# Output products of the first eight units of a fused retention and MoE kernel: one plain float32 matmul in place of three reduced-precision ones

## The chip, the cores and the metric

The kernel runs on one core of a Trainium2 chip. The metric is the time of one execution on the device in microseconds; the median of several runs is compared. The engines are TensorE (PE; its weight loads are PEld), VectorE (DVE), ScalarE (ACT), GpSimd (POOL) and SyncE (SP, which issues all DMAs). Each works through its own instructions in order and waits on semaphores for the others.

## The reference

Three layers follow one another. A retention layer over 4 sequences of 768 positions, 8 heads of 64 features, gives 3072 tokens of 512 features. Then come two feed-forward layers; the change is in the first of them:

```python
def _moe_ref(x, w_in, w_out):            # x 3072x512, w_in 512x2048, w_out 2048x512
    h = x @ w_in
    g = h * (1.0 / (1.0 + np.exp(-1.702 * h)))
    return (g @ w_out).astype(np.float32)
...
    gate = 1.0 / (1.0 + np.exp(-(x @ w_gate)))     # second layer, d_ff 1536
    return (gate * (x @ w_val) @ w_out).astype(np.float32)
```

The feed-forward weights come as float64 words in memory; the kernel turns them into float32 itself.

## The kernel before

The first feed-forward layer works on six blocks of 512 tokens and sixteen slices of 128 of the 2048 features. A pair of block and slice is a **unit**; there are 96. The list `units` orders them: block 0 with slices 0 to 7, block 1 with slices 0 to 7, block 0 with 8 to 15, block 1 with 8 to 15, and then blocks 2 to 5 with all sixteen each. `FH` is 8, so units 0 to 7 are block 0 with the first eight slices. The order of all instructions is written by hand.

The precise products are made of three matmuls in the reduced-precision type float32r: an operand is split into a high part (a cast on ScalarE) and a low part (the difference, on VectorE or GpSimd), and high times high, high times low and low times high are added up in PSUM. Weights are split anew for each unit: `split_w` casts `wh` on ScalarE (line 265) and subtracts `wl` on GpSimd or VectorE (line 266). The float32 weights themselves stay in `raw1` for the whole layer. Attention products (`emit_scores`, `emit_update`, `emit_y`) are plain float32 matmuls; the profile records each of these as two instructions.

One turn of the loop over units issues, for unit i:

1. `conv[0]`, `conv[1]`: the first steps of turning weight tiles from float64 to float32, two tiles per unit in units 0 to 7 and one in the next ones: a scaling on ScalarE (line 228, tile `cva`, three buffers), then on VectorE L233 and L236.
2. `proj`: twelve matmuls of 512 columns into a bank `h` (L273 to L275).
3. `split_for(i + 1)`: the next unit's input weights, `wh` on ScalarE and `wl` on GpSimd (on VectorE from unit 24).
4. `gated`: a sigmoid on ScalarE (L279, into `sg`), the product with `h` on VectorE (L280), and the cast of its high part `gh` on ScalarE (L283).
5. `split_out(i + 1)`: the output weights of unit i - 1, `wh` on ScalarE and `wl` on GpSimd.
6. `conv[2]`: L242 and L246 on VectorE.
7. One item of attention for the next block, if there is one. Units 0 to 5 have two items each for block 1. A step of attention (128 tokens) is three items: scores (L144, masked on VectorE at L148), state (L165), and the output (L178, L185, evicted to `xh` on ScalarE and `xl` on VectorE, L190), which also prepares `vs` and `qs` of the following step on GpSimd (L110, L118).
8. `gated_lo`: the low part `gl` on VectorE (L288).
9. `conv[3]`: the sum that ends the conversion, on GpSimd (L256, into `raw1`).
10. `stage`: loads of further weight tiles. Then the second item of attention.
11. `emit_out(i - 2)`: the output product of the unit before the last, twelve matmuls of 512 columns (L365 to L367), four banks `acc` that add up over eight slices.

The banks `h` are three, taken in turn by the projections and the attention items. The tiles `gh` and `gl` have three buffers each, `sg` two.

Of the kernel before, what the change touches and what calls it, by code (L numbers as in the profile page):

```python
# [8 lines left out]
F32 = mybir.dt.float32  # L9
# [6 lines left out]
P = 128  # L16
# [8 lines left out]
def retention_moe_moe2(  # L25
# [12 lines left out]
    nc = tc.nc  # L38
# [12 lines left out]
    def pool(stack, name, bufs, side, **kw):  # L51
        return stack.enter_context(tc.tile_pool(name=name, bufs=bufs, side=side, reuse_waits="tile", **kw))
# [5 lines left out]
    g_p = pool(left, "g", 2, "left")  # L58
# [10 lines left out]
    def psum_tile(kind, shape=(P, 512)):  # L69
        i = turn[kind][0]  # L70
        turn[kind].rotate(-1)
        return psum[i].tile(list(shape), F32, name=kind, tag="bank")
# [121 lines left out]
    raw1 = {}  # L194
# [7 lines left out]
    def stage(n=1):  # L202

        for _ in range(min(n, len(to_stage))):
            ph, f, k = to_stage.popleft()
            t = cv_p.tile([P, 512], U64, name="w64", tag="w64", bufs=4)
            nc.sync.dma_start(out=t, in_=(w1 if ph == "1" else w2)[f, k])
            staged.append((ph, f, k, t))
# [53 lines left out]
    def split_w(raw, lo_engine):  # L262
        wh = wsp_p.tile([P, 512], F32R, name="wh", tag="wh")
        wl = wsp_p.tile([P, 512], F32R, name="wl", tag="wl")
        nc.scalar.copy(wh, raw)  # L265
        lo_engine.tensor_tensor(out=wl, in0=raw, in1=wh, op=ALU.subtract)  # L266
        return wh, wl


    def proj(bank, w, xh, xl, n):  # L270
        wh, wl = (a.rearrange("p (k f) -> p k f", k=KC) for a in w)
        for k in range(KC):
            nc.tensor.matmul(bank[:, :n], wh[:, k, :], xh[:, k, :n], start=(k == 0), stop=False)  # L273
            nc.tensor.matmul(bank[:, :n], wh[:, k, :], xl[:, k, :n], start=False, stop=False)  # L274
            nc.tensor.matmul(bank[:, :n], wl[:, k, :], xh[:, k, :n], start=False, stop=(k == KC - 1))  # L275

    def gated(bank, n):
        sg = g_p.tile([P, 512], F32, name="sg", tag="sg")
        nc.scalar.activation(out=sg[:, :n], in_=bank[:, :n], func=AF.Sigmoid, scale=1.702)  # L279
        nc.vector.tensor_tensor(out=sg[:, :n], in0=bank[:, :n], in1=sg[:, :n], op=ALU.mult)  # L280
        gh = g_p.tile([P, 512], F32R, name="gh", tag="gh", bufs=3)
        gl = g_p.tile([P, 512], F32R, name="gl", tag="gl", bufs=3)
        nc.scalar.copy(gh[:, :n], sg[:, :n])  # L283
        return sg, gh, gl

    def gated_lo(g, n):
        sg, gh, gl = g
        nc.vector.tensor_tensor(out=gl[:, :n], in0=sg[:, :n], in1=gh[:, :n], op=ALU.subtract)  # L288

    x_t, w_t, g_t, acc_t, half_t = {}, {}, {}, {}, {}  # L290
# [4 lines left out]
    def att_items(j):  # L295

        t0, n = blocks1[j]
        items = []
        for i in range(n // C):
            s = t0 // C + i  # L300

            def first(s=s, i=i):
                if i == 0:
                    alloc_x(j)
                emit_scores(s)
                if s >= 3:
                    load_next(s + 1, KN, V)

            def second(s=s):
                emit_update(s)  # L310
                if s >= 3:
                    load_next(s + 2, Q, K)

            def third(s=s, i=i):
                if s + 1 < NSTEP:
                    emit_prep(s + 1)
                emit_y(s, *x_t[j], i * C)

            items += [first, second, third]
        return deque(items)  # L320
# [3 lines left out]
    FH = F1 // 2  # L324
    segments = [(b, f0, f0 + FH) for f0 in (0, FH) for b in range(2)]
    segments += [(b, 0, F1) for b in range(2, len(blocks1))]
    units = [(b, f) for b, f0, f1 in segments for f in range(f0, f1)]
    starts = {(b, f0) for b, f0, f1 in segments}
    ends = {(b, f1 - 1) for b, f0, f1 in segments}
    DEPTH = 2  # L330

    def split_out(i):

        j = i - DEPTH
        if 0 <= j < len(units):
            w_t[j, "out"] = split_w(raw1[units[j][1], 1], nc.gpsimd)

    def split_for(i):

        if i < len(units):  # L340
            b, f = units[i]
            w_t[i, 0] = split_w(raw1[f, 0], nc.gpsimd if i < 3 * FH else nc.vector)

    def half_tile(c):
        if c < 3:
            return in_p.tile([P, 512], F32, name="half", tag="half", bufs=3)
        return g_p.tile([P, 512], F32, name="ost", tag="ost")

    def emit_out(i):
        b, f = units[i]  # L350
        if (b, f) in starts:
            acc_t[b] = [psum_tile("acc") for _ in range(4)]
            if f:
                half_t[b] = []
                for c in range(4):
                    half_t[b].append(half_tile(c))
                    nc.sync.dma_start(out=half_t[b][c], in_=halfd[b][:, c, :])
        acc = acc_t[b]
        _, gh, gl = g_t.pop(i)
        wh, wl = w_t.pop((i, "out"))  # L360
        n = blocks1[b][1]
        st, sp = (b, f) in starts, (b, f) in ends
        for c in range(4):
            a, wc = acc[c][:, :n], slice(c * P, (c + 1) * P)
            nc.tensor.matmul(a, wh[:, wc], gh[:, :n], start=st, stop=False)  # L365
            nc.tensor.matmul(a, wl[:, wc], gh[:, :n], start=False, stop=False)  # L366
            nc.tensor.matmul(a, wh[:, wc], gl[:, :n], start=False, stop=sp)  # L367
        if not sp:
            return
        for c in range(4):  # L370
            t = half_t[b][c] if b in half_t else half_tile(c) if b < 2 else half_tile(3)
            if b in half_t:
                nc.vector.tensor_tensor(out=t, in0=acc[c], in1=half_t[b][c], op=ALU.add)
            elif c % 2:
                nc.scalar.copy(t, acc[c])
            else:
                nc.vector.tensor_copy(t, acc[c])  # L377
            nc.sync.dma_start(out=(x2d if f == F1 - 1 else halfd)[b][:, c, :], in_=t)
# [20 lines left out]
    def open_early():  # L399
        p2["x"] = pool(ctx, "x2", 1, "right")  # L400
        p2["xt"] = pool(ctx, "xt", 6, "right")
        p2["w"] = [pool(ctx, "we", 1, "right")]
# [58 lines left out]
    def load_chain(n):  # L461
        if n >= len(chains):
            return
        g, r, p, m = chains[n]
        f = 2 * (r * PAIRS + p)
        t = p2["w"][n % 2].tile([P, 8, 256], F32, name="raw8", tag="raw8")
        for ff, sl in ((f + 1, slice(A21, A22 + 1, 2)), (f, slice(A11, A12 + 1))):
            nc.sync.dma_start(out=t[:, sl, :], in_=w2d[ff, m].rearrange("p (a c) -> p a c", a=2))
        wraw8[n] = t
# [162 lines left out]
    with tc.manual_schedule():  # L632
# [54 lines left out]
        for i, (b, f) in enumerate(units):  # L687
            if i == 0:
                items = att_items(1)
            elif (b, f) == (1, FH):  # L690
                items = att_items(2)
            elif b > 1 and f == 0:
                items = att_items(b + 1) if b + 1 < len(blocks1) else deque()
                if b == len(blocks1) - 1:
                    assert not staged and not to_stage
                    right.close()
                    open_early()
                    xs = prep_x(0)
                    load_chain(0)
            first = staged and staged[0][0] == "1"  # L700
            conv = [lambda: None] * 4
            if first:
                conv = convert(2 if i < FH else 1, nc.gpsimd)
            elif staged and (5 * i) // 8 > (5 * (i - 1)) // 8:
                conv = convert(1, nc.vector)
            xh, xl = x_t[b]
            n = blocks1[b][1]
            conv[0]()
            conv[1]()
            hb = psum_tile("h")  # L710
            proj(hb, w_t.pop((i, 0)), xh, xl, n)
            if i > 0:
                split_for(i + 1)
            g_t[i] = gated(hb, n)
            split_out(i + 1)
            conv[2]()
            if items and (b < 2 or f >= 1):
                items.popleft()()
            gated_lo(g_t[i], n)
            conv[3]()  # L720
            stage(4 - len(staged))
            if items and b < 2:
                items.popleft()()
            pend.append(i)
            while pend and i - pend[0] >= DEPTH:
                emit_out(pend.popleft())
            next(xs, None)
            if b == len(blocks1) - 1:
                if f == 9:
                    sums(0)  # L730
                elif f in (11, 13):
                    split_chain(0, f == 13)()
# [141 lines left out]
```

## Time and profile before

| | |
|---|---|
| median of 3 runs | 1252.93 us (1251.56 to 1253.75) |
| profiled execution | 1253.17 us, span 1251.2 us |
| TensorE busy | 1196.4 us (96%) |
| VectorE busy | 826.2 us (66%) |
| GpSimd busy | 552.2 us (44%) |
| ScalarE busy | 545.8 us (44%) |
| granted TensorE clock, mean | 0.989 of full speed |

The span is what the profiler saw of the instructions; the execution's own time has some 2 us around it. Busy shares are means over the whole span, and the stages differ: the first 200 us hold the start of the attention and all conversions of the first layer's weights. "L266" is line 266 of the kernel. In the views an arrow "<-" in brackets names what ended an engine's idle time, with the us of waiting ahead of it.

### The profile page before, as it was taken

Reading aid. Unit: us, or ns where it says so; the run is one execution under the profiler, and the core shown is the slowest. Engines: PE = TensorE matmul, PEld = TensorE weight load, DVE = VectorE, ACT = ScalarE, POOL = GpSimd, SP = SyncE. Lnnn points to the kernel's source line nnn. Section 1 sums busy time; section 2 is a strip of 40 time slices with the busy share of each in tenths; the row PEclk is TensorE's granted clock in tenths of the full one; section 3 lists DMA queues with packets and bytes.
Section 4 is the critical chain, followed back from the end, with each engine's and each line's share of the span. In section 5 each row is a group of like instructions: output and inputs, shape, how many; then the busy total and the mean of one; then the engine's idle time right before and its main releaser. Section 6 shows DMA issues by size and latency. Waiting matters only on the chain.

```text
span 1251.2 us, 16113 instructions
## 1 busy us (share of the span) xinstructions
PE 1196.4 (96%) x5948; PEld 959.4 (77%) x5948; DVE 826.2 (66%) x1057; ACT 545.8 (44%) x964; POOL 552.2 (44%) x406
## 2 busy tenths in 40 slices
PE   6888999999999999999998999999999999999998
PEld 5666767887788888788786787877787877787877
DVE  5999998787777777875772536466535457535454
ACT  5344444344344444443553526163625253525251
POOL 4777774423332332322454625256525256634330
PEclk9889999999999999999999999999999999999999
DMA  8553343543424434402102202033212123211111
GB/s 296 201 169 104 115 152 118 187 166 121 129 88 156 142 110 134 132 24 85 48 1 84 76 26 76 26 93 119 92 35 69 33 74 128 86 51 51 51 34 68
DMA packets 62431, 123.49 MB, mean 99 GB/s; under 512 B 6800, under 2 KB 16016, under 8 KB 62352
## 3 DMA queue, kind: packets, MB, share of 16 engines
q1 hardware_dynamic: 62352, 122.46, 30.0%
q8 instruction: 47, 0.77, 0.3%
q14 instruction: 32, 0.26, 0.1%
HBM read 98.31 MB, written 24.12 MB: 98 GB/s over the span
## 4 chain that ended last, share of the span: by engine, by line
PE 69%; issue 7%; POOL 7%; DVE 5%; ACT 3%; DMA 1%; SPq 0%; POOLq 0%; DVEq 0%; ACTq 0%
PE pa L497 15%; PE acc L365 5%; PE pd L497 5%; PE acc L366 5%; PE acc L367 5%; PE h L275 5%; PE h L274 5%; PE h L273 5%; PE po L615 4%; PE po L614 4%; PE po L613 4%; POOL wl L266 3%; PE pb L497 3%; POOL wraw L256 2%; DVE g2l L527 1%
## 5 line engine op out<-in xcount | busy, mean ns | idle before, releaser
L266 POOL TENSOR_TENSOR wl<-wraw,wh 128x512 fp32r<-128x512 f32 x120 | 176.4, 1471 | 345.4 <-ACT wh L265 324.6
L366 PE MATMUL acc<-gh,wl 128*128 128x512 f32 x384 | 152.9, 398 | 8.0 <-POOL wl L266 8.0
L365 PE MATMUL acc<-gh,wh 128*128 128x512 f32 x384 | 156.5, 408 | 1.5 <-DVE half L377 0.8
L275 PE MATMUL h<-xh,wl 128*128 128x512 f32 x384 | 152.6, 397 | 2.7 <-POOL wl L266 2.6
L273 PE MATMUL h<-xh,wh 128*128 128x512 f32 x384 | 152.2, 396 | 2.8 <-DVE xl L190 1.1
L274 PE MATMUL h<-xl,wh 128*128 128x512 f32 x384 | 151.9, 396 | 0.2 <-DVE xl L190 0.2
L367 PE MATMUL acc<-gl,wh 128*128 128x512 f32 x384 | 151.0, 393 | 0.0
L279 ACT ACTIVATE sg<-h 128x512 f32<-128x512 f32 x96 | 57.4, 598 | 189.3 <-PE h L275 189.2
L489 POOL TENSOR_TENSOR ol<-raw,oh 128x768 fp32r<-128x768 f32 x36 | 66.8, 1857 | 154.8 <-ACT oh L486 154.8
L497 PE MATMUL pa<-xoh,oh 128*128 128x512 f32 x288 | 115.7, 402 | 16.6 <-ACT u L556 11.7
L265 ACT CAST wh<-wraw 128x512 fp32r<-128x512 f32 x192 | 116.4, 614 | 0.2
L283 ACT CAST gh<-sg 128x512 fp32r<-128x512 f32 x96 | 59.6, 621 | 128.5 <-DVE sg L280 128.5
L497 PE MATMUL pa<-xoh,ol 128*128 128x512 f32 x288 | 114.0, 396 | 0.8 <-DVE ol L489 0.8
L497 PE MATMUL pa<-xol,oh 128*128 128x512 f32 x288 | 114.3, 397 | 0.0
L613 PE MATMUL po<-woh,g2h 128*128 128x512 f32 x288 | 112.5, 391 | 1.1 <-DVE ost L506 1.1
L614 PE MATMUL po<-wol,g2h 128*128 128x512 f32 x288 | 112.5, 391 | 0.0
L615 PE MATMUL po<-woh,g2l 128*128 128x512 f32 x288 | 112.5, 390 | 0.0
L280 DVE TENSOR_TENSOR sg<-h,sg 128x512 f32<-128x512 f32 x96 | 65.9, 686 | 55.8 <-ACT sg L279 55.8
L288 DVE TENSOR_TENSOR gl<-sg,gh 128x512 fp32r<-128x512 f32 x96 | 82.6, 860 | 17.2 <-ACT gh L283 17.2
L366 PEld LDWEIGHTS acc<-gh,wl 128*128 128x128 f32 x384 | 72.9, 190 | 26.1 <-POOL wl L266 12.3
L365 PEld LDWEIGHTS acc<-gh,wh 128*128 128x128 f32 x384 | 72.8, 190 | 23.7 <-issue 3.0
L275 PEld LDWEIGHTS h<-xh,wl 128*128 128x128 f32 x384 | 72.7, 189 | 22.2 <-POOL wl L266 5.5
(111 smaller groups left out, 2502.5 us busy)
## 6 DMA issues: line engine op xcount, KB each, us to landing
w<-in_w_dram SPq DMA_DIRECT2D x68, 512.0 KB, 3.6
in_t<-in_qkv_dram SPq DMA_DIRECT2D x96, 256.0 KB, 3.7
raw<-w2d SPq DMA_DIRECT2D x72, 256.0 KB, 3.1
w2d<-cva SPq DMA_DIRECT2D x36, 256.0 KB, 2.2
wor<-w2d SPq DMA_DIRECT2D x36, 256.0 KB, 2.7
xt<-x2d SPq DMA_DIRECT2D x24, 256.0 KB, 4.3
out_dram<-ost SPq DMA_DIRECT2D x24, 256.0 KB, 2.0
x2d<-ost SPq DMA_DIRECT2D x18, 256.0 KB, 2.8
```

Of the source, the lines that this page charges most:

```text
L265: nc.scalar.copy(wh, raw)
L266: lo_engine.tensor_tensor(out=wl, in0=raw, in1=wh, op=ALU.subtract)
L273: nc.tensor.matmul(bank[:, :n], wh[:, k, :], xh[:, k, :n], start=(k == 0), stop=False)
L274: nc.tensor.matmul(bank[:, :n], wh[:, k, :], xl[:, k, :n], start=False, stop=False)
L275: nc.tensor.matmul(bank[:, :n], wl[:, k, :], xh[:, k, :n], start=False, stop=(k == KC - 1))
L365: nc.tensor.matmul(a, wh[:, wc], gh[:, :n], start=st, stop=False)
L366: nc.tensor.matmul(a, wl[:, wc], gh[:, :n], start=False, stop=False)
L367: nc.tensor.matmul(a, wh[:, wc], gl[:, :n], start=False, stop=sp)
L497: nc.tensor.matmul(bank, w[:, kk], x[:, k, :], start=start and k == 0 and w is wh and x is xh, stop=stop and k == 1 and w is wl, skip_grou ...
L613: nc.tensor.matmul(bank, gh, wh, start=f == 0, stop=False)
L614: nc.tensor.matmul(bank, gh, wl, start=False, stop=False)
L615: nc.tensor.matmul(bank, gl, wh, start=False, stop=f == FR - 1)
```

## The change

In units 0 to 7 the output weights are no longer split and the gated value is no longer split. `gated` writes the sigmoid into a tile `gw` that takes the three buffers of `gh`, multiplies it there and returns it; the cast `gh` and the difference `gl` are left out, and so are `wh` and `wl` of those units' output weights. The output product of such a unit is one plain float32 matmul per bank instead of three float32r ones, from the float32 weights in `raw1` and from `gw`. All other units are as before.

```diff
-    def gated(bank, n):
-        sg = g_p.tile([P, 512], F32, name="sg", tag="sg")
+    def gated(bank, n, whole):
+
+        if whole:
+            sg = g_p.tile([P, 512], F32, name="gw", tag="gh", bufs=3)
+        else:
+            sg = g_p.tile([P, 512], F32, name="sg", tag="sg")
         nc.scalar.activation(out=sg[:, :n], in_=bank[:, :n], func=AF.Sigmoid, scale=1.702)
         nc.vector.tensor_tensor(out=sg[:, :n], in0=bank[:, :n], in1=sg[:, :n], op=ALU.mult)
+        if whole:
+            return (sg,)
...
     def gated_lo(g, n):
+        if len(g) == 1:
+            return
...
+    WHOLE = FH
+
     def split_out(i):
 
         j = i - DEPTH
-        if 0 <= j < len(units):
+        if WHOLE <= j < len(units):
             w_t[j, "out"] = split_w(raw1[units[j][1], 1], nc.gpsimd)
...
-        _, gh, gl = g_t.pop(i)
-        wh, wl = w_t.pop((i, "out"))
+        g = g_t.pop(i)
...
         for c in range(4):
             a, wc = acc[c][:, :n], slice(c * P, (c + 1) * P)
+            if i < WHOLE:
+                nc.tensor.matmul(a, raw1[f, 1][:, wc], g[0][:, :n], start=st, stop=sp)
+                continue
+            _, gh, gl = g
+            wh, wl = w_t[i, "out"]
             nc.tensor.matmul(a, wh[:, wc], gh[:, :n], start=st, stop=False)
             nc.tensor.matmul(a, wl[:, wc], gh[:, :n], start=False, stop=False)
             nc.tensor.matmul(a, wh[:, wc], gl[:, :n], start=False, stop=sp)
+        w_t.pop((i, "out"), None)
...
-            g_t[i] = gated(hb, n)
+            g_t[i] = gated(hb, n, i < WHOLE)
```

## Rows read from the trace of the kernel before

**Rows 1.** Busy us by stage; columns PE, PEld, DVE, ACT, POOL, clock, DMA, GB/s:

```profile
48.00:109.00 61.00, 51.37 (x285) 39.78 (x283) 57.29 (x71) 24.49 (x45) 45.11 (x30) 0.91 0.47 155
109.00:197.00 88.00, 81.91 (x336) 63.27 (x336) 85.97 (x90) 39.99 (x73) 67.00 (x44) 0.98 0.39 125
197.00:1251.20 1054.20, 1029.89 (x4997) 828.95 (x4995) 648.44 (x845) 457.79 (x795) 415.87 (x312) 1.00 0.27 86
```

**Rows 2.** VectorE in order of time, units 2 to 10; start, us, instruction:

```profile
54.73 0.68 DVE L280 TENSOR_TENSOR sg<-h,sg 128x512 f32<-128x512 f32 x1
...
60.88 0.97 DVE L233 TENSOR_SCALAR cva<-cva 128x512 uint32<-128x512 uint32 x1 [0.45 <-ACT cva L228]
61.76 3.22 DVE L236 SCALAR_TENSOR_TENSOR cva<-w,cva 128x512 uint32<-128x512 uint32 x2
64.90 0.68 DVE L280 TENSOR_TENSOR sg<-h,sg 128x512 f32<-128x512 f32 x1
65.50 0.75 DVE L242 TENSOR_SCALAR cvb<-cva 128x512 uint32<-128x512 uint32 x2
66.17 1.28 DVE L246 SCALAR_TENSOR_TENSOR cvb<-w,cvb 128x512 f32<-128x512 uint32 x2
...
68.58 0.67 DVE L288 TENSOR_TENSOR gl<-sg,gh 128x512 fp32r<-128x512 f32 x1
...
85.86 0.68 DVE L280 TENSOR_TENSOR sg<-h,sg 128x512 f32<-128x512 f32 x1
...
105.85 0.68 DVE L280 TENSOR_TENSOR sg<-h,sg 128x512 f32<-128x512 f32 x1
...
120.12 0.68 DVE L280 TENSOR_TENSOR sg<-h,sg 128x512 f32<-128x512 f32 x1
...
125.60 0.68 DVE L280 TENSOR_TENSOR sg<-h,sg 128x512 f32<-128x512 f32 x1
```

**Rows 3.** GpSimd in order of time, units 2 and 3:

```profile
52.20 1.46 POOL L266 TENSOR_TENSOR wl<-wraw,wh 128x512 fp32r<-128x512 f32 x1
...
62.70 1.73 POOL L266 TENSOR_TENSOR wl<-wraw,wh 128x512 fp32r<-128x512 f32 x1
66.89 1.73 POOL L266 TENSOR_TENSOR wl<-wraw,wh 128x512 fp32r<-128x512 f32 x1 [2.46 <-issue]
68.57 3.22 POOL L256 TENSOR_TENSOR wraw<-cva,cvb 128x512 f32<-128x512 f32 x2
```

**Rows 4.** TensorE in order of time, units 1 to 8:

```profile
44.94 1.41 PE L144 MATMUL h<-in_t 64*128 64x128 f32 x14 [2.90 <-DVE sg L280]
47.41 0.80 PE L273 MATMUL h<-xh,wh 128*128 128x512 f32 x1 [1.07 <-DVE xl L190]
...
52.63 1.05 PE L178 MATMUL h<-qs,R 128*128 128x128 f32 x8
53.61 1.09 PE L185 MATMUL h<-A,in_t 128*64 128x128 f32 x16
54.63 0.50 PE L365 MATMUL acc<-gh,wh 128*128 128x512 f32 x1
...
57.49 0.40 PE L273 MATMUL h<-xh,wh 128*128 128x512 f32 x1
...
60.40 1.16 PE L144 MATMUL h<-in_t 64*128 64x128 f32 x16
62.79 0.69 PE L165 MATMUL st<-vs,in_t 128*64 128x64 f32 x16 [1.24 <-POOL vs L110]
...
75.00 2.07 PE L144 MATMUL h<-in_t 64*128 64x128 f32 x14 [4.32 <-DVE sg L280]
...
110.52 0.79 PE L366 MATMUL acc<-gh,wl 128*128 128x512 f32 x1 [2.26 <-POOL wl L266]
```

**Rows 5.** Groups by line, 44 to 110 us: busy and mean ns, idle before:

```profile
L266 POOL TENSOR_TENSOR wl<-wraw,wh 128x512 fp32r<-128x512 f32 x13 | 21.9, 1685 | 19.3 <-issue 15.0 <-ACT wh L265 3.4 <-POOL wl L266 0.8
...
L288 DVE TENSOR_TENSOR gl<-sg,gh 128x512 fp32r<-128x512 f32 x7 | 9.0, 1286 | 0.0
```

## The prediction

> **What bounds the kernel now.** I read the busy time by stage first [rows 1]. From 197 us to the end TensorE is busy 1029.89 of 1054.2 us, so nothing that is done earlier can shorten that stage; it can only start it sooner. Every touched unit lies before it. In 48 to 109 us, where units 2 to 8 run (the first sigmoid is unit 0's, one unit follows another), TensorE is busy 51.37 of 61 us, VectorE 57.29, GpSimd 45.11, ScalarE 24.49: VectorE is nearly full. From 109 to 197 us VectorE is fuller still (85.97 of 88), and nothing there is edited. So the question is how much earlier unit 9 or 10 reaches its place; from there the old pace goes on.
>
> Then the instructions of VectorE and GpSimd in unit 3 [rows 2, 3] show why VectorE is full. The pair on line 236 takes 3.22 us while GpSimd is in a `wl` and its neighbours; the pair on line 246, with GpSimd idle until 66.89, takes 1.28. A VectorE instruction on SBUF operands waits while a GpSimd instruction runs. VectorE's busy time is thus partly GpSimd's.
>
> The loop that sets the pace goes through both: VectorE multiplies the gate (L280 at 64.90), makes the low half of the converted weights (L242, L246, the first ending near 66.8), GpSimd adds the two (L256), ScalarE scales the next tile into the freed `cva` buffer, then VectorE's L233, two L236 and the next L280. The row at 60.88 shows the release of L233 by ScalarE's `cva`. But GpSimd starts L256 only at 68.57, because the output weights' `wl` is queued before it and runs from 66.89 [rows 3]: it starts late, since its `wh` is cast behind the cast of the gated value, which waits for L280. So 68.57 - 66.8 = 1.75 us of every turn are the output weights' split. The turn: 1.9 (L280 to the first L246's end) + 1.75 + 1.6 (L256) + 0.7 (scaling) + 4.0 (60.88 to 64.90) = 10.0 us, against (105.85 - 54.73) / 5 = 10.2 from the L280 rows.
>
> TensorE's rows [rows 4] show a loose second limit: it waits 2.9 us before 44.94 and 4.3 before 75.00 for L280 (the scores need the bank that L280 reads), 2.3 before 110.52 for `wl`, and 1.07 before 47.41. After such waits its matmuls are slow: from 47.41 the twelve of unit 2's projection take until 52.63, 5.2 us against 2.9 for twelve in 57.49 to 60.40.
>
> **The change, part by part.** Removed: eight `wl` on GpSimd (mean 1.69), eight `gl` on VectorE (mean 1.29 with their waits), 16 casts on ScalarE [rows 5]. ScalarE's casts are worth nothing by themselves: it is busy 24 of 61 us [rows 1]. The `wl` is worth its 1.75 per turn. The `gl` lies behind L246 and before the next turn's first L233, which waits for nothing else that is late; with `wl` kept it would be worth about nothing. With `wl` gone it would be next in line, and it goes too. The new turn is 10.0 - 1.75 = 8.25 us.
>
> Where a unit also has `vs` or `qs` on GpSimd, these stood behind `wl` or L256; they now start sooner. No DMA, no buffer count and no queue order is changed. The gated value takes the buffers of `gh`, three as before: unit i reuses that of unit i-3, whose product precedes projection i on TensorE, so no new wait.
>
> Added: TensorE's product. Before, twelve reduced-precision matmuls took 54.63 to 57.49, 2.86 us [rows 4]. After, four plain float32 ones of 512 columns. The trace has none of that size. The nearest row is L178, plain float32, 128x128 by 128 columns: four matmuls stand as eight records, 52.63 to 53.61, 0.98 us, or 0.245 each. Upper bound: four times that, 0.98. Lower: a record at 128 columns takes 0.1225, and 256 cycles at 2.4 GHz (the granted clock is 0.91 of it over the stretch, with the slow parts in it [rows 1]) are 0.107; without any fixed part 512 columns in two records take 0.85. I take 0.107 x 4 + 0.016 per record, 0.89 a matmul and 3.6 us a unit: 0.75 more than now, six us over eight units, on an engine that waits now but will wait less.
>
> So the saving is not 8 x 1.75 = 14. I walk the units, taking for each L280 the later of two routes: VectorE's (previous + 8.25) and TensorE's (the items in between, a product 3.6, a projection 2.9, sigmoid and hand-over 0.7). A step of attention costs TensorE 1.05 (scores), 0.62 (state), 2.0 (L178 and L185 together); two thirds of one falls to a unit up to unit 5.
> Unit 1: nothing moves; L280 of unit 0 and of unit 1 stand behind conversions that GpSimd holds up as before. TensorE's wait and its slow stretch after it remain.
> Unit 2: the slow projection ends at 52.6, so L280 starts near 53.5 against 54.73.
> Unit 3: TensorE's product from 54.63 to 58.2, projection to 61.1, L280 at 61.8; VectorE's route also 61.75. Before 64.90.
> Unit 4: scores and state to 62.8, product to 66.4, projection to 69.3, VectorE 70 plus some port waits for `vs` and `qs`: 71. TensorE's 4.3 us wait before 75.00 shrinks to about 1, and I expect no slow stretch after it.
> Unit 5: rest of the scores to 72.4, product, projection to 79, L280 at 80.5 with VectorE's own items. Before 85.86.
> Unit 6: state and attention to 82, product and projection to 88.6, L280 at 89.3.
> Unit 7, with no attention: VectorE's turn, 97.5. Before 105.85.
> Unit 8, one tile to convert: 102.6.
> Unit 9: TensorE no longer waits for `wl` (the 2.3 us and the slow stretch after 110.52): 101.6 + 6.5 + 0.6 = 108.8 against 120.12.
> Unit 10: 115.2 against 125.60.
> The last two give 11.3 and 10.4: I take 11 us. After that every instruction is the old one at the old pace, and TensorE's full stage begins 11 us sooner. The profiled execution took 1253.17 us around a span of 1251.2; less 11 it is 1242.2, and the profiled time lies 0.24 above the median of the runs, so 1242.0.
>
> **The rivals.** *The port is all that counts.* Eight `wl` at 1.46 us (the shortest kind, at 52.20 [rows 3]) plus eight `gl` of 0.67 (at 68.58 [rows 2]) then leave one serial resource: 8 x 2.1 = 17 us, 1236. For it: VectorE at 57.29 of 61. Against: by the walk TensorE is due within a us of VectorE in units 3 to 6. The Trainium skill's page "SBUF — State Buffer" ("SBUF: two separate sides") calls the ports that VectorE and GpSimd share an exclusive lock, held for a whole instruction; the 3.22 against 1.28 agrees, and by that rule alone this rival would be the forecast.
> *TensorE becomes the bound.* At 0.98 a matmul the six products up to unit 8 cost 2.2 us more, and if the wait in unit 4 still lasts long enough to slow it, some ten matmuls at 0.43 instead of 0.23 cost 2.3 more: a gain of 6, 1247. For it: it has only 61 - 51.37 = 9.6 us of waits to fill in the stretch. The Trainium skill, "FP8 and Floating Point Precision" ("TensorE Precision Notes"), counts four passes for true float32, where the split has three matmuls. At 0.24 a pass (2.86 / 12) that would be 0.95 a matmul, 1.5 us less gained over 24 matmuls.
> *Slower: plain float32 runs at the lower clock.* If the long matmuls left TensorE at 1.2 GHz through units 2 to 9, a matmul would take 1.7 us, the product 6.9 and the projection 5.2. Between the projections of units 1 and 8 stand seven projections (20.3 us), ten thirds of a step of attention (12.2) and the waits and the slow stretch that remain before unit 2 (2.9 before 44.94, 1.07 before 47.41, 2.3 of slowing [rows 4]; 6.3): 39 us of the 68 that these units take now. So 29 us are left for 24 matmuls, and above 1.2 us each the kernel loses. At 1.7 it is 24 x 1.7 + 39 - 68 = 12 us slower before the projections' own slowing, 1265. Against: L178 is plain float32 and stands between fast matmuls.
> *No change.* The gain is made and lost again, because 109 to 197 us is paced by a load from memory and not by the engines: 1253. Against: VectorE is busy 85.97 of 88 there.
>
> **Chances.** Forecast (8.5 to 13.5 us gained) 0.62; port alone (14 to 17) 0.13; TensorE (3 to 8) 0.15; no change 0.04; slower 0.06. 0.2%, 2.5 us, is what a measurement of this kernel tells from no change. Faster is the sum of the first three, 0.90. The range 1237 to 1248 takes in the forecast's own, 1239 to 1244, a part of the port rival and most of TensorE's; the bounds of the matmul's price (0.85 to 0.98, together 4 us over 32) lie within it.
>
> **What would show it.** In the profile after: a turn of about 8.3 us between the L280 of units 2 to 7; L256 starting within 0.2 us of the first L246's end; the new matmul as two records of about 0.44 each; the wait before unit 4's scores near 1 us and its clock full; the start of unit 9's product with no wait; and the same pace after 110 us, everything shifted by 11. It is wrong if GpSimd's `wl` of the input weights moves into the place of the one removed, if TensorE's record is longer than 0.5 us, or if a slow stretch appears at a new place.

## The result, and the profile after

The changed kernel takes 1238.52 us (median of 4 runs, 1237.37 to 1239.93) against 1252.66 us of the kernel before (4 runs beside it): ratio 0.9888, 95% interval 0.9873 to 0.9903, 14.1 us faster. The prediction was 1242.0, with 1237 to 1248 as its range. The profiled execution after has a span of 1235.6 us, 15.6 less than the one before.

Busy time by stage, columns as in [rows 1]; the first stretch is that of [rows 1], the second ends where TensorE's full stage begins:

```profile
48.00:109.00 61.00, 60.49 (x286) 38.86 (x286) 55.94 (x74) 21.33 (x38) 40.86 (x27) 0.96 0.51 180
109.00:183.00 74.00, 69.55 (x292) 53.77 (x292) 72.42 (x76) 35.25 (x65) 54.80 (x36) 1.00 0.41 128
```

TensorE, which had 9.6 us of waits in the first of these, has 0.5, and the same 61 us now hold the multiplications of eight units (2 to 9) instead of six (2 to 7).

VectorE, to be laid beside [rows 2]; the gate's multiplication is line 284 now:

```profile
53.68 0.69 DVE L284 TENSOR_TENSOR gw<-h,gw 128x512 f32<-128x512 f32 x1 [1.53 <-ACT gw L283]
...
59.00 3.22 DVE L236 SCALAR_TENSOR_TENSOR cva<-w,cva 128x512 uint32<-128x512 uint32 x2
62.15 0.68 DVE L284 TENSOR_TENSOR gw<-h,gw 128x512 f32<-128x512 f32 x1
62.75 0.75 DVE L242 TENSOR_SCALAR cvb<-cva 128x512 uint32<-128x512 uint32 x2
63.42 1.28 DVE L246 SCALAR_TENSOR_TENSOR cvb<-w,cvb 128x512 f32<-128x512 uint32 x2
...
70.74 0.68 DVE L284 TENSOR_TENSOR gw<-h,gw 128x512 f32<-128x512 f32 x1
...
79.74 0.69 DVE L284 TENSOR_TENSOR gw<-h,gw 128x512 f32<-128x512 f32 x1 [0.67 <-ACT gw L283]
...
96.55 0.68 DVE L284 TENSOR_TENSOR gw<-h,gw 128x512 f32<-128x512 f32 x1
...
107.88 0.68 DVE L284 TENSOR_TENSOR sg<-h,sg 128x512 f32<-128x512 f32 x1
...
114.53 0.68 DVE L284 TENSOR_TENSOR sg<-h,sg 128x512 f32<-128x512 f32 x1
```

Unit 2 starts its multiplication at 53.68, unit 7 at 96.55: 8.6 us a turn instead of 10.2. Unit 9 is 12.2 us early, unit 10 11.1. GpSimd in unit 3, beside [rows 3]:

```profile
59.95 1.73 POOL L266 TENSOR_TENSOR wl<-wraw,wh 128x512 fp32r<-128x512 f32 x1
64.17 3.21 POOL L256 TENSOR_TENSOR wraw<-cva,cvb 128x512 f32<-128x512 f32 x2 [2.50 <-DVE cvb L246]
```

L256 starts at 64.17, right after the first L246 (near 64.06), with nothing queued before it. TensorE, beside [rows 4]:

```profile
54.89 3.70 PE L375 MATMUL acc<-gw,wraw 128*128 128x512 f32 x8
58.03 0.80 PE L273 MATMUL h<-xh,wh 128*128 128x512 f32 x1
58.66 0.40 PE L274 MATMUL h<-xl,wh 128*128 128x512 f32 x1
...
71.47 1.16 PE L144 MATMUL h<-in_t 64*128 64x128 f32 x14 [0.51 <-DVE gw L284]
...
100.51 3.59 PE L375 MATMUL acc<-gw,wraw 128*128 128x512 f32 x8
```

The new product is eight records. It runs 3.14 us to the first row of the next projection, and that row is 0.63 us ahead of the next instead of 0.23: 3.5 us in all. The wait before unit 4's scores is 0.51 us (4.32 before), and the product at 100.51, that of unit 6, which is issued in the turn of unit 8, follows the projection without a wait (2.26 before).

From unit 24 on every unit stands 11.4 to 12.2 us earlier. The rest of the difference between the two profiles comes long after, where the first layer gives way to the second: there the lead grows from 11.8 us to 15.6. TensorE's row there, first of the kernel before, then of the changed one; the eighth value is the clock:

```profile
680.00:692.00 12.00, 8.68 (x28) 6.11 (x27) 2.77 (x3) 6.01 (x9) 8.24 (x8) 0.81 0.39 133
```

```profile
668.00:680.00 12.00, 9.17 (x38) 6.52 (x37) 4.12 (x6) 6.00 (x10) 8.53 (x8) 1.00 0.38 132
```

In the profile of before TensorE falls to 1.2 GHz for 6.8 us after a few waits of 0.7 to 1.9 us; in that of after it does not, with waits of 0.7 to 1.4. Work done at half the clock for 6.8 us is late by 3.4, an estimate from these rows that is most of the 3.8.

### The profile page after: what moved, and what is told of

Same layout as the page of the kernel before. It is cut to its first block, busy times and chain, and to the rows that moved or that the text cites. A ratio compares the mean times of both kernels' runs of the same rounds, so it can differ in the third digit from the quotient of the medians.

```text
span 1235.6 us, 15997 instructions
## 1 busy us (share of the span) xinstructions
PE 1191.6 (96%) x5916; PEld 947.7 (77%) x5916; DVE 815.1 (66%) x1049; ACT 537.8 (44%) x948; POOL 537.4 (43%) x398
## 4 chain that ended last, share of the span: by engine, by line
PE 73%; DVE 10%; issue 6%; POOL 4%; ACT 3%; DMA 3%; SPq 1%; POOLq 0%; DVEq 0%; ACTq 0%
PE pa L512 15%; PE acc L379 5%; PE pd L512 5%; PE h L275 5%; PE h L273 5%; PE h L274 5%; PE acc L380 5%; PE acc L381 5%; PE po L630 4%; PE po L629 4%; PE po L628 4%; PE pb L512 3%; DVE cva L236 2%; PE acc L375 2%; DVE g2l L542 1%
## 5 line engine op out<-in xcount | busy, mean ns | idle before, releaser
L266 POOL TENSOR_TENSOR wl<-wraw,wh 128x512 fp32r<-128x512 f32 x112 | 161.4, 1442 | 327.7 <-ACT wh L265 321.8
L380 PE MATMUL acc<-gh,wl 128*128 128x512 f32 x352 | 138.8, 394 | 4.8 <-POOL wl L266 4.8
L379 PE MATMUL acc<-gh,wh 128*128 128x512 f32 x352 | 142.4, 405 | 0.8 <-ACT sg L283 0.8
L381 PE MATMUL acc<-gl,wh 128*128 128x512 f32 x352 | 137.3, 390 | 0.0
L265 ACT CAST wh<-wraw 128x512 fp32r<-128x512 f32 x184 | 111.5, 614 | 0.2
L289 ACT CAST gh<-sg 128x512 fp32r<-128x512 f32 x88 | 54.6, 621 | 101.8 <-DVE sg L284 101.8
L284 DVE TENSOR_TENSOR sg<-h,sg 128x512 f32<-128x512 f32 x88 | 60.5, 687 | 54.4 <-ACT sg L283 54.4
L273 PEld LDWEIGHTS h<-xh,wh 128*128 128x128 f32 x384 | 72.8, 189 | 21.1 <-DVE xl L190 1.5
L274 PEld LDWEIGHTS h<-xl,wh 128*128 128x128 f32 x384 | 72.7, 189 | 18.1 <-issue 1.9
L296 DVE TENSOR_TENSOR gl<-sg,gh 128x512 fp32r<-128x512 f32 x88 | 71.8, 816 | 17.2 <-ACT gh L289 17.2
```

## The experiments

The clean measure is the distance between the gate multiplications of two units in one profile, in us; the start of a profile moves by up to 2 us with slow stretches of TensorE in the first 30 us (unit 2 of the changed kernel starts at 53.68 in one profile and at 55.77 in another). For the kernel before unit 2 to 7 is 105.85 - 54.73 = 51.12. The ratio is to runs of the kernel before beside each; their medians lie between 1251.59 and 1252.94.

| kernel | unit 2 to 7 | 2 to 9 | 2 to 24 | median us | ratio to before, 95% |
|---|---|---|---|---|---|
| before | 51.12 | 65.39 | 155.44 | 1252.66 | |
| changed | 42.87 | 54.20 | 144.41 | 1238.52 | 0.9888 (0.9873 to 0.9903) |
| wl kept | 50.58 | 63.07 | 153.02 | 1248.99 | 0.9976 (0.9964 to 0.9987) |
| gl kept | 44.89 | 57.05 | 147.41 | 1244.24 | 0.9942 (0.9925 to 0.9958) |
| both kept | 51.38 | 65.59 | 155.79 | 1252.53 | 1.0008 (0.9998 to 1.0017) |
| high parts only | 43.52 | 55.13 | 145.13 | 1240.82 | 0.9914 (0.9895 to 0.9933) |
| wl kept, behind | 46.68 | 59.07 | 149.71 | 1246.09 | 0.9950 (0.9935 to 0.9964) |
| before, wl behind | 51.15 | 64.30 | 152.41 | 1249.24 | 0.9974 (0.9964 to 0.9984) |
| changed, wl behind | 42.84 | 54.18 | 142.44 | 1238.45 | 0.9898 (0.9874 to 0.9921) |
| plain to unit 21 | 42.85 | 53.79 | 146.92 | 1241.32 | 0.9915 (0.9896 to 0.9934) |
| every second unit | 42.84 | 53.79 | 142.18 | 1238.21 | 0.9889 (0.9873 to 0.9905) |
| other banks | 46.06 | 57.50 | 147.70 | 1240.97 | 0.9907 (0.9883 to 0.9930) |

**One part undone at a time.** First the weights' split, kept and not read:

```diff
-        if WHOLE <= j < len(units):
+        if 0 <= j < len(units):
             w_t[j, "out"] = split_w(raw1[units[j][1], 1], nc.gpsimd)
```

> The output weights of units 0 to 7 are split as before, but nothing reads the parts; the product stays plain float32 and the gated value unsplit. My theory (GpSimd's wl stands in the loop): the turn goes back to about 10 us, the gate's multiplication of unit 7 starts at 105 us (before 105.85, changed kernel 96.55); only TensorE's wait for wl in unit 8 stays gone, so 1248 to 1251 us. Rival (the port, every instruction counts by its length): removing gl alone still gives 0.67 us a unit, unit 7 at 101.8 us, 1244 us.

Unit 7 starts at 105.33: without `gl` alone the five turns are 0.5 us shorter, not 3.4. The median is 1248.99, inside what my theory gave; the port rival's 1244 is out. The reason that my theory gave for the time does not hold, though: units 7 to 9 take 12.49 us instead of 14.27, and the run with both splits kept, below, lacks TensorE's wait in unit 8 as well and gains nothing there, so this is the work of the missing `gl`. And the rows show that `wl` is no longer where I had put it. GpSimd in unit 3 of this run:

```profile
62.11 3.41 POOL L266 TENSOR_TENSOR wl<-wraw,wh 128x512 fp32r<-128x512 f32 x2
66.81 3.21 POOL L256 TENSOR_TENSOR wraw<-cva,cvb 128x512 f32<-128x512 f32 x2 [1.30 <-DVE cvb L246]
```

Both `wl` run together at 62.11, since the cast that waited for the gate is gone from ScalarE's queue. L256 waits for L246 and for nothing else. The turn is nearly as long as ever (64.31 to 73.60, 9.29 us; 9.37 before): `wl` now holds up VectorE (L242 takes 1.23 us here, 0.75 in [rows 2]).

Then the gated value's split, kept and not read:

```diff
         if whole:
-            return (sg,)
+            gh = g_p.tile([P, 512], F32R, name="gh", tag="sg")
+            gl = g_p.tile([P, 512], F32R, name="gl", tag="gl", bufs=3)
+            nc.scalar.copy(gh[:, :n], sg[:, :n])
+            return sg, gh, gl
...
-        if len(g) == 1:
-            return
```

> The gated value of units 0 to 7 is split as before (cast on ScalarE, difference on VectorE), but nothing reads the parts; the weights stay unsplit. My theory: most of the gain remains, since gl is ahead of a step that waits 0.35 to 0.47 us per turn anyway; unit 7's multiplication at 98 to 100 us (changed kernel 96.55), 1240 to 1242 us. Rival (the port): gl costs its length plus the GpSimd instruction it waits for, 1.3 us a unit, unit 7 at 104.4 us, 1247 us.

Unit 7 starts at 99.62. With `wl` gone, `gl` costs (44.89 - 42.87) / 5 = 0.4 us a turn and 2.85 us up to unit 9: inside what my theory gave for unit 7 (98 to 100), but at 1244.2 us between the two theories in time. `wl` is the larger part, but `gl` is not free.

Then both:

> Both splits are done as before and not read; only TensorE's product is the plain one. My theory: TensorE's longer product is hidden while the turn is 10 us, unit 7's multiplication at 105 to 106 us, and the wait for wl in unit 8 is gone: 1249 to 1252 us. Rival (TensorE is the bound): each product's extra 0.7 us shows, unit 7 at 110 us, 1255 us or more.

It has the edits of both runs above. Unit 7 at 106.28, unit 9 at 120.49 and 1252.53 us: TensorE's longer product costs nothing that can be measured (51.38 against 51.12), so it is hidden while both splits are there, and the TensorE rival is out. Beside the two runs above, `wl` is worth 51.38 - 44.89 = 6.5 us over the five turns with `gl` kept and 50.58 - 42.87 = 7.7 without it, 1.3 to 1.5 a turn. One step of mine is out as well: TensorE's wait for `wl` in unit 8 is gone in this run, and unit 9 is as late as before. VectorE there, behind a row of the kernel before at the same place:

```profile
112.18 1.49 DVE L242 TENSOR_SCALAR cvb<-cva 128x512 uint32<-128x512 uint32 x1 [0.57 <-POOL wraw L256]
```

```profile
111.39 0.68 DVE L284 TENSOR_TENSOR sg<-h,sg 128x512 f32<-128x512 f32 x1
112.62 1.48 DVE L242 TENSOR_SCALAR cvb<-cva 128x512 uint32<-128x512 uint32 x1 [0.56 <-POOL wraw L256]
...
120.49 0.68 DVE L284 TENSOR_TENSOR sg<-h,sg 128x512 f32<-128x512 f32 x1
```

After unit 8's multiplication VectorE waits for GpSimd's L256, which `wl` had delayed (2.65 us long, from 108.26), and five of its instructions then take 1.5 to 1.8 us each. The kernel before has the same wait. Unit 9 was held by VectorE and GpSimd all along, and not by TensorE.

**A shorter product.** Only the high parts, one matmul per bank:

```diff
-            return (sg,)
+            gh = g_p.tile([P, 512], F32R, name="gh", tag="gl", bufs=3)
+            nc.scalar.copy(gh[:, :n], sg[:, :n])
+            return (gh,)
...
-        if WHOLE <= j < len(units):
+        if 0 <= j < WHOLE:
+            wh = wsp_p.tile([P, 512], F32R, name="wh", tag="wh")
+            nc.scalar.copy(wh, raw1[units[j][1], 1])
+            w_t[j, "out"] = wh
+        elif WHOLE <= j < len(units):
...
-                nc.tensor.matmul(a, raw1[f, 1][:, wc], g[0][:, :n], start=st, stop=sp)
+                nc.tensor.matmul(a, w_t[i, "out"][:, wc], g[0][:, :n], start=st, stop=sp)
```

> Units 0 to 7 leave out the low parts: one float32r matmul of the high parts per bank (the output lacks their low parts), with the two casts on ScalarE, no wl and no gl; TensorE's product shrinks from 3.1 to about 1 us. My theory: VectorE's turn still sets the pace, only the waits for the sigmoid in units 5, 6 and 8 (0.67, 0.62, 0.20 us) go: unit 9's multiplication at 106 to 106.5 us (changed kernel 107.88), 1237 us. Rival (TensorE became the bound): 2 us a unit less, unit 9 before 100 us, 1230 us or less.

Both are wrong: unit 2 to 9 takes 55.13 us, 0.9 longer than with the plain product, though TensorE has some 2.5 us a unit less to do. Its stage row shows that TensorE used the room for waits:

```profile
48.00:109.00 61.00, 46.77 (x251) 35.32 (x252) 56.62 (x73) 28.06 (x51) 40.82 (x28) 0.87 0.52 177
```

TensorE is busy 46.77 us instead of 60.49, and its mean clock falls from 0.96 to 0.87: around a wait of 3.97 us in unit 4 it falls to 1.2 GHz for 6.8 us, and around one of 3.10 us in unit 9's projection for 3.4. With the plain product the first of these waits is 0.51 us and the second is not there. But the clock is little of the 0.9 us. Behind unit 2 the multiplications wait for a sigmoid only in unit 5, 0.84 us (0.67 in the changed kernel), and some 0.1 us in unit 9. The time is lost in units 5 to 6 (9.75 us against 9.17) and 7 to 8 (5.57 against 4.79), on VectorE:

```profile
84.70 0.69 DVE L190 TENSOR_TENSOR xl<-h,xh 128x512 fp32r<-128x512 f32 x1 [0.59 <-ACT xh L189]
...
101.33 1.51 DVE L233 TENSOR_SCALAR cva<-cva 128x512 uint32<-128x512 uint32 x1
102.88 1.63 DVE L236 SCALAR_TENSOR_TENSOR cva<-w,cva 128x512 uint32<-128x512 uint32 x1
104.43 0.68 DVE L284 TENSOR_TENSOR sg<-h,sg 128x512 f32<-128x512 f32 x1
```

In unit 5 VectorE waits 0.59 us (0.16 in the changed kernel) for ScalarE's `xh`, which stands behind the two casts that this run adds. In unit 7 its L233 takes 1.51 us instead of 0.42 (GpSimd is in L256 both times), and unit 8's multiplication waits for nothing. So the run shows that the shorter product gains nothing, as VectorE sets the pace; it does not show that the lower clock makes it slower.

**The same work in another place.** The run with `wl` kept, with that split issued behind L256:

```diff
-            split_out(i + 1)
+            if i > FH:
+                split_out(i + 1)
             conv[2]()
...
             conv[3]()
+            if i <= FH:
+                split_out(i + 1)
```

> As the run with wl kept, but the unread split of the output weights in units 0 to 8 is issued behind the sum that ends the conversion instead of ahead of it: the same work on GpSimd, only out of the loop's way. My theory (what counts is that wl stands ahead of the sum): most of the gain comes back, the multiplication of unit 7 at 97.5 to 100 us, 1240 to 1242 us. Rival (the port: GpSimd's total counts): unit 7 at 104 to 105.5 us as in that run, 1248 us.

Between the two: five turns take 46.68 us, 3.9 less than with `wl` ahead and 3.8 more than without it. And the move alone, in the kernel before (`first` holds in units 0 to 20), with the precise product:

```diff
-            split_out(i + 1)
+            if not first:
+                split_out(i + 1)
             conv[2]()
...
             conv[3]()
+            if first:
+                split_out(i + 1)
```

> The kernel before, precise products in all units, with the same move of the split of the output weights in units 0 to 20. My theory: half of wl's effect was its place: 4 us in units 2 to 9 and 3 in the next twelve, 1245 to 1247 us. Rival (TensorE then waits for the later wl, or the port's load alone counts): 1252 us or more.

1249.24 us, some 3 less than before, where 5 to 7 were expected, and not where I said: units 2 to 7 take 51.15 us, the same as before; 1.1 us are gained to unit 9 and 3.0 to unit 24. VectorE and GpSimd in its unit 3:

```profile
64.88 0.68 DVE L280 TENSOR_TENSOR sg<-h,sg 128x512 f32<-128x512 f32 x1
...
69.15 2.90 DVE L233 TENSOR_SCALAR cva<-cva 128x512 uint32<-128x512 uint32 x2
71.97 3.19 DVE L236 SCALAR_TENSOR_TENSOR cva<-w,cva 128x512 uint32<-128x512 uint32 x2
75.09 0.68 DVE L280 TENSOR_TENSOR sg<-h,sg 128x512 f32<-128x512 f32 x1
```

```profile
66.91 3.46 POOL L256 TENSOR_TENSOR wraw<-cva,cvb 128x512 f32<-128x512 f32 x2 [2.50 <-DVE cvb L246]
70.32 2.85 POOL L266 TENSOR_TENSOR wl<-wraw,wh 128x512 fp32r<-128x512 f32 x2
```

VectorE in that turn of the kernel before:

```profile
72.00 2.35 DVE L236 SCALAR_TENSOR_TENSOR cva<-w,cva 128x512 uint32<-128x512 uint32 x2
74.27 0.68 DVE L280 TENSOR_TENSOR sg<-h,sg 128x512 f32<-128x512 f32 x1
```

L256 starts 1.66 us earlier than in [rows 3], and yet the turn takes 10.21 us where it took 9.37: the pair of L233 ends when it ended before (72.05 against 72.08), now with L256 and `wl` beside it, and L236, beside the second `wl` and the `vs` that GpSimd runs from 73.13, takes 3.19 us instead of 2.35. The next turn gives the time back (10.74 us, 11.59 before). TensorE, which waits for the later `wl` in the rival, has little part in it: in units 2 to 7 only unit 5's multiplication waits for its sigmoid, 0.71 us. So `wl` does not cost its 1.75 us by its place. With `gl` kept it costs as much in the other place; with `gl` gone, its place is worth half.

The same move in the changed kernel:

> The changed kernel, with the split of the output weights issued behind the sum that ends the conversion in every unit that converts first-layer weights (so units 9 to 20). My theory: wl's place in the loop also paces that stage: 0.3 us a unit less over 12 units, 3 to 4 us less than the changed kernel, 1234.5 to 1236 us. Rival (there the port's load alone sets the pace): 1238.5 us.

It takes the edit just shown. From unit 2 to 24 it gains 2.0 us over the changed kernel (142.44 against 144.41), but its median is 1238.45, the same. The move does speed up units 9 to 20 there; in the time it is within what runs of one kernel differ.

**How far it can be carried.** Plain products to unit 21 (`WHOLE = 22`):

> The plain product and the unsplit gated value in units 0 to 21 instead of 0 to 7. A unit with a plain product takes TensorE 6.2 us (97.34 to 103.54 in the changed kernel), the old pace of units 10 to 21 is 12.35 us for two. My theory: VectorE and GpSimd get free, TensorE becomes the bound at the same pace, no gain over the changed kernel: 1237 to 1240 us, TensorE without a wait in 110 to 185 us. Rival (the port is the bound and TensorE has room): 0.9 us a unit more, 1226 us.

Unit 9 to 21 takes 74.4 us (107.77 to 182.18; changed kernel 74.25): the same pace. The stage of 110 to 182 us, first the changed kernel, then this run:

```profile
110.00:182.00 72.00, 67.55 (x285) 52.55 (x284) 70.42 (x73) 34.09 (x62) 53.67 (x36) 1.00 0.42 132
```

```profile
110.00:182.00 72.00, 72.00 (x236) 44.25 (x235) 42.91 (x61) 21.69 (x39) 36.42 (x24) 1.00 0.43 132
```

VectorE goes from 70.42 to 42.91 us and nothing gets faster, because TensorE has no wait left. The median, 1241.32, is 1.3 us above what I expected: the last two long products stand where the changed kernel already runs at its shorter pace.

Then in every second unit of 8 to 21:

```diff
-    WHOLE = FH
+    def is_whole(i):
+        return i < FH or (i < 22 and i % 2 == 0)
...
```

> Plain in units 0 to 7 and in the even ones of 8 to 21. My theory: TensorE's mean need is (6.2 + 5.45) / 2 = 5.8 us a unit against the pace of 6.18, VectorE's and GpSimd's mean need falls below that: 14 x 0.35 = 5 us less than the changed kernel, 1233.5 us. Rival (what is freed is taken up by contention): 1238 us.

Unit 2 to 21 takes 124.69 us against 128.45, 3.8 less of the 5 expected; at unit 24 2.2 are left, and the median is 1238.21, not 1233.5. TensorE is busy 72.00 of 72 us between 110 and 182 us, so it is the limit again, and long products that end there are paid for. No version here beats the changed kernel by more than its runs differ.

**TensorE's wait in unit 1.**

```diff
         banks.clear()
-        banks.append("h")
+        banks.append("acc")
...
+            if i == 2:
+                banks.clear()
+                banks.append("h")
```

> The changed kernel with the attention items of units 0 and 1 in the four accumulation banks, which are unused until unit 2, so that TensorE doesn't wait 3.4 us in unit 1 for the gate's multiplication. My theory: unit 2's projection is no longer slow, its multiplication starts at 52.2 instead of 53.68 us, and the waits for the sigmoid in units 5 and 6 go: 1.5 to 3 us less than the changed kernel, 1235.5 to 1237 us. Rival: TensorE's wait is only moved behind the projection, to the mask of unit 1's scores on VectorE, and the clock falls all the same: 1238.5 us.

The rival holds, and worse. TensorE's waits in this run:

```profile
49.99 0.43 PE L185 MATMUL h<-A,in_t 128*64 128x128 f32 x2 [2.42 <-DVE A L148]
...
71.69 2.07 PE L144 MATMUL h<-in_t 64*128 64x128 f32 x14 [2.38 <-DVE gw L284]
73.69 6.00 PE L375 MATMUL acc<-gw,wraw 128*128 128x512 f32 x8
79.13 0.80 PE L273 MATMUL h<-xh,wh 128*128 128x512 f32 x1
```

```profile
83.15 0.69 DVE L284 TENSOR_TENSOR gw<-h,gw 128x512 f32<-128x512 f32 x1 [3.92 <-ACT gw L283]
```

The first is the wait moved behind the projection. TensorE, earlier by then, waits 2.38 us in unit 4 where it had waited 0.51, and is at 1.2 GHz from there on for 6.8 us; the plain product runs 5.4 us to the next projection instead of 3.1, and unit 5's multiplication waits 3.92 us for the sigmoid (0.67 in the changed kernel). Unit 2 to 7 takes 46.06 us instead of 42.87. An earlier TensorE was a slower one in this profile. It is of the slowest of the four executions (1243.29 us; the fastest took 1237.17), so the fall need not be in all of them.

**Both kernels once more.**

> The kernel before once more, for a second profile. If the slow stretch of TensorE at the change of layers (690 to 700 us, 6.8 us at the lower clock) belongs to the kernel, it is there again; if it falls by chance of the run, it is there in some profiles of either kernel. My theory: chance; the multiplications of units 2 to 24 stand at the same distances as before within 0.3 us, 155.4 us from unit 2 to 24.

> The changed kernel once more, for a second profile. My theory: 144.4 us from unit 2's multiplication to unit 24's, within 0.3 us of its first profile; the stretch at the change of layers may or may not be slow. Rival: the changed kernel never has it, and 3.4 us of its gain are caused there.

Unit 2 to 24: 155.43 and 144.50 us, within 0.1 of the first profiles; the 11 us are the kernels'. The spans, 1250.7 and 1239.1 us, differ by 11.6 here, where those of the first two differ by 15.6; unit 0 of the changed kernel alone starts 2.1 us later than in its first profile (37.64, 35.56). The slow stretch at the change of layers is there again in the kernel before, half as long, and again not in the changed kernel. Over all fourteen profiles it is there in seven (both of before, both kept, every second unit, other banks, `wl` kept behind, before with `wl` behind) and not in the other seven; the same few waits stand there with it and without. Whether the change has a part in it is open.

## Why the prediction was right

The change took the time where the prediction said, in units 2 to 9, by some 11 us, and kept it. The time alone would not show this: the 14.1 us measured lie above the forecast's own 8.5 to 13.5, just inside the port rival's 14 to 17, and are what the rejected 8 x 1.75 gives. It is the units' starts that bear the forecast out. By its own steps:

**The walk held.** Its starts of L280 for units 2 to 10 (53.5, 61.8, 71, 80.5, 89.3, 97.5, 102.6, 108.8, 115.2) were measured as 53.68, 62.15, 70.74, 79.74, 88.91, 96.55, 101.34, 107.88, 114.53. Taking the later of two routes for every unit was the step that kept it from the port rival's 17 us. (In its sum for unit 9, 101.6 + 6.5 + 0.6 is 108.7, and where the 101.6 comes from is not said; the product started at 100.51. In the TensorE rival ten matmuls at 0.20 us more are 2.0, not 2.3. Neither changes a chance.)

**TensorE's price held**: 3.5 us a product against 3.6. The walk has TensorE's route as the later one about units 4 to 6; in the run the multiplications of units 5 and 6 do wait for their sigmoid, 0.67 and 0.62 us. Where the turn is longer, the product is hidden (both kept: no change). The Trainium skill, "FP8 and Floating Point Precision" ("TensorE Precision Notes"), has four passes for true float32. At the 0.23 us of a float32r matmul here that would be 0.92 us a matmul, an estimate; 3.5 / 4 is 0.88, so the trace roughly agrees. What I did not say is that TensorE's granted clock is higher with the longer product: 0.96 in 48 to 109 us against 0.87 with the high parts only. What a fall can cost, the run with other banks shows: 3.2 us in one turn (unit 4 to 5 takes 12.20 us instead of 9.00).

**What failed is the reason given for the 1.75 us a turn**, "68.57 - 66.8 = 1.75 us of every turn are the output weights' split" standing ahead of L256. Moved out of the way it saves nothing in units 2 to 7 of the kernel before, and 3.9 of 7.7 us once `gl` is gone. The rows of that run show what is gained at L256 spent again by L236 beside the moved `wl` and what GpSimd runs behind it. What the runs show in its place is that VectorE and GpSimd take turns: `wl` is worth 1.3 to 1.5 us a turn and `gl` 0.1 to 0.4 more, and the two together shorten the turn by 1.65 (51.12 to 42.87 over five turns), where 1.75 was forecast. That the place gave nearly the same number as the load was luck. That `gl` would be next in line once `wl` is gone was right (0.4 us). The port rival was wrong the other way: it would have `gl` alone worth 0.67 a turn, and it is 0.1 in units 2 to 7 and 2.3 us in all up to unit 9.

**Unit 9 was right in size for a wrong reason.** It is not TensorE's wait for `wl` (both kept has none, and unit 9 is at 120.49) but that of VectorE for GpSimd: units 7 to 9 take 14.2 us with both splits kept, 12.5 without `gl`, 12.2 without `wl` and 11.3 without either.

**The 3.5 us that are missing** between 1242.0 and 1238.5 lie mostly outside the walk: at units 9 and 10 it was 0.8 us too slow, and the slow stretch at the change of layers, where 3.8 us came on top in the first two profiles and 1.4 in the second two, is not in the profiles after. No step spoke of it, and whether the change has a part in it is not shown.

## What to carry to other kernels

When two engines take turns on a port, an instruction's price is not read from the place where it holds up the other: move it before believing that, and count what both do in a turn. An engine with waits in a stage that others pace can take over their work at little or no cost, even at more work in all; this ends, as the run to unit 21 shows, where it has no wait left. Walk the units with both routes: the starts came out within 1.3 us and the lead as 11, where 11.8 was kept up to the change of layers; a price per unit times their number gives 14. And take more than one pair of profiles: the same two kernels differ by 15.6 us in the first pair and by 11.6 in the second.

## What the runs showed of the hardware

That GpSimd can be the one that waits. In unit 3 of the run with `gl` kept, VectorE and GpSimd:

```profile
68.08 0.75 DVE L233 TENSOR_SCALAR cva<-cva 128x512 uint32<-128x512 uint32 x2
68.75 1.28 DVE L236 SCALAR_TENSOR_TENSOR cva<-w,cva 128x512 uint32<-128x512 uint32 x2
```

```profile
65.83 5.33 POOL L256 TENSOR_TENSOR wraw<-cva,cvb 128x512 f32<-128x512 f32 x2 [3.10 <-DVE cvb L246]
```

VectorE's four instructions take 2.0 us here, and GpSimd's pair 5.33 instead of 3.2. The Trainium skill, "SBUF — State Buffer" ("SBUF: two separate sides"), says that whichever starts first holds the shared ports for its whole instruction; in [rows 2] it was GpSimd, here it is VectorE, and the order changed with one instruction more on VectorE and a cast more on ScalarE.

And that less work on TensorE went with a lower clock and no gain: a granted clock of 0.87 in 48 to 109 us and 55.13 us for units 2 to 9 with 1 us a product, 0.96 and 54.20 with 3.5.
